# Seven products instead of eight in the first matrix product of the last 1,024 tokens, with the operand sums of two token groups on GpSimd

## The chip, the cores and the metric

The kernel runs on one core of a Trainium2 chip. The core has a matrix engine (TensorE, "PE" in the profile), a vector engine (VectorE, "DVE"), a scalar engine (ScalarE, "ACT"), GpSimd ("POOL") and SyncE ("SP"), all of which run their own instruction streams and meet through semaphores. SBUF is the working memory with 128 partitions, PSUM holds the results of matmuls in eight banks of 128 x 512 float32. DMAs are issued from the queues of POOL, SP and ACT. The metric is the device time of one execution in microseconds (us).

## The reference, cut to what matters

Windowed attention over 8 batches, 8 heads, 576 positions and 64 values a head, and then a two-layer network over all 4,608 tokens:

```python
scores = scale * np.matmul(q, k.transpose(0, 1, 3, 2))
mask = np.abs(pos[:, None] - pos[None, :]) <= 32
scores = np.where(mask, scores, -1000000000.0)
attn = softmax(scores)
x = np.matmul(attn, v).transpose(0, 2, 1, 3).reshape(4608, 512)
h = x @ w_in                # 512 -> 2048: the first product
g = np.maximum(h, 0.0) ** 2
out = g @ w_out             # 2048 -> 512: the second product
```

Inputs and output are float32; the kernel computes in bfloat16 with float32 sums.

## The kernel before, in words

**Attention.** The 576 positions of a batch are cut into three blocks of 192 queries; there are 24 blocks G = 0 to 23. For each block q, k and v are loaded by POOL (`load_qk`, `load_v`, L365 and L396; these DMAs turn float32 into bfloat16), two pieces each. q and k are then transposed: on PE for the first two batches (`turn_pe`, L432), by DMA transposes from SP's queue afterwards (`turn_dma`, L452). `scores` (L489) multiplies them into PSUM region AT, ACT takes the exponential (L510), DVE multiplies by the window's mask (L515), `pv` (L535) multiplies with v, and DVE divides by the row sum (L550, L553). In the first three blocks the mask is added on PE instead (L480). `xturn` transposes the result into the ring XT, on PE for six blocks, by DMA from SP after that (L584, L587).

**First product.** `mm1` (L605) takes a token tile of 192, 256 or 512 tokens and one or two column tiles of 128 of the 2,048, four matmuls for each, into one of two PSUM banks HT. ACT applies relu (L611), DVE squares (L614) into the ring GT. A tile can start only when XT holds all its tokens. Before, tiles have 192 tokens up to 768, 256 up to 1,024 and 512 after that.

**Second product.** For the first 512 tokens it is done plainly (`mm2`, L625). From there on it works in groups g = 1 to 8 of 512 tokens by Strassen's scheme (`strassen`, `product`, L687): seven products P1 to P7 of half size instead of eight. Each is issued as two halves, "a" and "b", of eight matmuls of 256 columns. The operands' sums are made beforehand: those of W2 once (`sums_w2`, L648), those of the tokens for each group (`sums_g`, L663: four sums in two parts, eight DVE instructions of 128 x 1024). The partial results are put together by ACT and DVE (L698, L715, L721, L723, L725), and ACT's queue stores them (L707). There is one set of three sum buffers SS, so the sums of one group wait for the products of the group before; the third sum is written over a quarter of GT.

**The order of the work.** Every operation is recorded by `Prog.rec` with what it reads and writes, a duration that the author booked, and a key. `Prog.schedule` then goes through all engines in simulated time, takes on each the ready operation with the lowest key, and so fixes the order on each engine; DMA queues have booked speeds, shares and slacks (`serve`). Keys come from the token position plus per-block offsets (OG for attention, OL for loads, OS for the second product's groups); DVE's and ACT's keys are taken from when PE needs them (`late`, BIAS). Gaps on PE before 40 us are filled with idle matmuls on zeros (L294). Nothing in the program orders engines apart from the semaphores that follow from reads and writes, and each engine works strictly in the order written down. Loads of batches 2 and later wait for a matmul recorded just before them (`after=self.moe`). The first loads stand in the list `opening()`: the first k by SP, one q by ACT, the others by POOL.

Of the kernel before, what the change touches and what calls it, by code (L numbers as in the profile page):

```python
# [21 lines left out]
BIAS = 74.0  # L22
LS = 10.75
OG = [-0.75, -0.25, -2.0, -2.75, -0.25, 2.25, 4.0, 1.25, 2.0, 1.75, 3.0, 0.75, 0.25, -0.25, -0.5, 0.25, -0.5, -2.0, -2.25, -3.0, 2.75, 1.25, -4.25, 3.0]
OL = [3.0, 1.0, 4.5, 5.5, 2.5, -0.5, -2.0, -3.5, -3.5, -0.5, 0.0, -0.5, -1.0, -3.5, -1.5, 1.5, -0.5, -3.5, -3.5, -1.0, 2.0, 1.0, -3.0, -6.5]
OS = [-4.0, 4.5, -2.0, 2.0, 1.75, 3.25, 4.5, 5.25, 4.5]
NV, NRAW = 6, 6
NTURN = 2
NXT = 6
LEAD = 10.0  # L30
# [5 lines left out]
NSPLIT = 6  # L36
NPM = 3
# [12 lines left out]
class Prog:  # L50
# [11 lines left out]
    def rec(self, eng, fn, reads=(), writes=(), dma=None, dur=100, key=0.0, move=0, name="", after=None, slack=0):  # L62
# [10 lines left out]
        for t in writes:  # L73
            w = self.writer.get(t)
            if w is not None:
                (op.order if w.eng == eng and w.dma is None and dma is None else op.deps).add(w)
            for r in self.readers.get(t, ()):
                (op.order if r.eng == eng and r.dma is None else op.deps).add(r)
# [13 lines left out]
    def schedule(self):  # L92
# [11 lines left out]
        for op in reversed(ops):  # L104
# [3 lines left out]
            if op.eng in ("ACT", "DVE") and op.dma is None and op.key > -50:  # L108
                op.key = op.late / 1000 - BIAS
# [20 lines left out]
        def serve(until):  # L130
            nonlocal now, spent
            while now < until:
# [10 lines left out]
                if spent >= (120 if now < 30000 else 180 if q == "POOL" else 60):  # L143
# [98 lines left out]
def act(n):  # L242
    return 175 + 0.833 * n
# [5 lines left out]

class Gen:  # L250
# [5 lines left out]
    def alloc(self):  # L256
        nc = self.nc
        sb, ps = nc.alloc_sbuf_tensor, nc.alloc_psum_tensor
        self.AT = ps("at", [128, 2048], F32)
        self.HT = [ps(f"ht{i}", [128, 512], F32) for i in range(2)]  # L260
        self.OUTP = [ps(f"outp{i}", [128, 512], F32) for i in range(2)]
# [10 lines left out]
        self.PT = [sb(f"pt{i}", [128, 8, 128], BF16) for i in range(3)]  # L272
# [9 lines left out]
        self.UE = [sb(f"ue{i}", [128, 512], F32) for i in range(2)]  # L282
        self.RT = [sb(f"rt{i}", [128, 512], BF16) for i in range(4)]
# [73 lines left out]
    def load_qk(self, t, b, g, key):  # L357
# [6 lines left out]
        for j in range(2):  # L364
# [4 lines left out]
    def load_hw(self, t, g, eng, cast, key):  # L369
# [4 lines left out]
        for j in range(2):  # L374
            u = 2 * (t == "q") + j
            if g == 0:
                f, tag = self.OE[u][0:h, :], ("oe", u)
            else:
                x = 4 * (g - 1) + u
                f, tag = self.W2[:, 2 * x:2 * x + 2, :].rearrange("p k c -> p (k c)").bitcast(F32)[0:h, :], ("w2f", x)  # L380
# [461 lines left out]
```

## Time and profile before

| | us |
|---|---|
| median of 3 runs (307.56 to 314.36) | 310.13 |
| the profiled execution, whole | 312.76 |
| its span, first to last instruction | 310.8 |
| PE busy | 292.8 |
| DVE busy | 192.6 |
| ACT busy | 166.7 |
| POOL busy | 117.6 |
| mean granted clock of TensorE | 0.995 |

The page divides the span into busy time by engine and by groups of instructions with the same line; an engine's matmul row "x8" stands for eight matmuls in a row, and "idle before" with the name of what ended it. In the view by stage each row is a stretch of the span: its bounds and length, and then the busy time (and number of instructions) of PE, of PE's weight loads, of DVE, ACT and POOL, the granted clock (1.00 is full speed), the share of the DMA engines, and GB/s. POOL's busy time in the kernel before is the issuing of loads, apart from a few small set-up instructions; its last load is issued at 210.5 us.

### The profile page before, as it was taken

What the parts mean: (1) busy time and instruction counts of PE and PEld (TensorE: products, weight loads), DVE (VectorE), ACT (ScalarE), POOL (GpSimd) and SP (SyncE); (2) the same over time, 40 slices, a digit from 0 to 9 for tenths busy, and PEclk for the clock granted to TensorE, in tenths of its full rate; (3) what the DMA queues carried; (4) which work ended last, traced back from release to release, by engine and by line L of the source; (5) the groups of instructions that cost most, each with busy time, mean ns of one, the idle gap of its engine ahead of it and who ended that gap; (6) DMA issues with size and microseconds to landing.
All of it is one profiled execution on the core that took longest, in us unless ns stands there. A gap on an engine that the chain in (4) does not pass through costs nothing.

```text
span 310.8 us, 7401 instructions
## 1 busy us (share of the span) xinstructions
PE 292.8 (94%) x2993; PEld 205.6 (66%) x3027; DVE 192.6 (62%) x420; ACT 166.7 (54%) x260; POOL 117.6 (38%) x153
## 2 busy tenths in 40 slices
PE   6899999999799999999999499999979999999995
PEld 6788776868685567556667455586548556666874
DVE  7135766645986896598539636695549765743701
ACT  3546657747536765746675156625762575355230
POOL 8999457308355650299114002992000000000000
PEclk9999999999999999999999979999999999999999
DMA  9999999999999999999999922999974311201123
GB/s 150 167 206 197 187 153 155 190 170 135 143 169 199 157 161 163 94 151 146 173 144 145 210 41 60 123 156 193 169 97 62 88 41 24 71 34 36 64 71 103
DMA packets 179553, 40.37 MB, mean 130 GB/s; under 512 B 166720, under 2 KB 179008, under 8 KB 179520
## 3 DMA queue, kind: packets, MB, share of 16 engines
q0 software_dynamic: 121920, 18.98, 92.7%
q1 hardware_dynamic: 46752, 11.09, 28.1%
q10 hardware_dynamic: 10848, 9.83, 11.4%
q8 instruction: 24, 0.39, 0.5%
q14 instruction: 9, 0.07, 0.1%
HBM read 38.80 MB, written 9.44 MB: 155 GB/s over the span
## 4 chain that ended last, share of the span: by engine, by line
PE 68%; issue 10%; DMA 8%; POOL 6%; DVE 4%; ACT 1%; SPq 1%; POOLq 0%; ACTq 0%; DVEq 0%
PE ht L605 30%; PE outp L687 23%; DMA kraw<-in_k_dram 5%; PE outp L625 4%; PE at L535 4%; PE at L489 3%; POOL kraw L365 2%; POOL qraw L365 2%; POOL v L396 2%; DMA v<-in_v_dram 2%; DMA qt<-qraw 2%; PE outp L294 2%; DVE ss L663 1%; DVE gt L614 1%; ACT rt L611 1%
## 5 line engine op out<-in xcount | busy, mean ns | idle before, releaser
L605 PE MATMUL ht<-xt,w 128*128 128x512 bf16 (+2 forms) x741 | 136.8, 326 | 6.1 <-issue 4.6
L611 ACT ACTIVATE rt<-ht 128x512 bf16<-128x512 f32 (+1 forms) x152 | 86.5, 576 | 74.4 <-PE ht L605 65.4
L605 PEld LDWEIGHTS ht<-xt,w 128*128 128x128 bf16 x768 | 68.6, 98 | 48.7 <-issue 5.6
L614 DVE TENSOR_TENSOR gt<-rt 128x512 bf16<-128x512 bf16 (+1 forms) x152 | 61.5, 408 | 59.0 <-ACT rt L611 56.6
L365 POOL DMA_DIRECT2D kraw<-in_k_dram x46 | 36.2, 809 | 92.6 <-issue 47.6
L510 ACT ACTIVATE e<-at 128x1024 bf16<-128x1024 f32 x42 | 41.4, 1021 | 11.0 <-PE at L489 11.0
L396 POOL DMA_DIRECT2D v<-in_v_dram x48 | 41.5, 891 | 0.1
L515 DVE TENSOR_TENSOR pt<-e,mask 128x1024 bf16<-128x1024 bf16 x42 | 29.0, 691 | 18.3 <-ACT e L510 18.2
L365 POOL DMA_DIRECT2D qraw<-in_q_dram x46 | 36.3, 810 | 0.5 <-issue 0.5
L687 PE MATMUL outp<-w,gt 128*128 128x256 bf16 x256 | 32.2, 273 | 0.7 <-ACT outp L698 0.7
L687 PE MATMUL outp<-ts,ss 128*128 128x256 bf16 x256 | 31.7, 273 | 0.3 <-DVE ss L663 0.3
L687 PE MATMUL outp<-ts,gt 128*128 128x256 bf16 x256 | 31.6, 273 | 0.0
L687 PEld LDWEIGHTS outp<-w,gt 128*128 128x128 bf16 x256 | 24.7, 98 | 7.7 <-ACT outp L698 1.1
L687 PEld LDWEIGHTS outp<-ts,ss 128*128 128x128 bf16 x256 | 24.4, 98 | 5.9 <-DVE ss L663 0.4
L687 PEld LDWEIGHTS outp<-ts,gt 128*128 128x128 bf16 x256 | 24.6, 98 | 4.2
L535 PEld LDWEIGHTS at<-v,pt 128*64 128x64 bf16 (+1 forms) x576 | 17.1, 106 | 12.6 <-issue 4.2
L535 PE MATMUL at<-v,pt 128*64 128x65 bf16 (+1 forms) x576 | 20.8, 196 | 2.8 <-DVE xa L553 1.7
L550 DVE RECIPROCAL rs<-at 64x8 f32<-64x8 f32 (+1 forms) x48 | 10.0, 209 | 15.3 <-PE at L535 14.0
L489 PEld LDWEIGHTS at<-qt,kt 64*128 64x128 bf16 x384 | 10.8, 94 | 11.1 <-issue 10.5
L489 PE MATMUL at<-qt,kt 64*128 64x128 bf16 x384 | 15.9, 218 | 1.8 <-DMA qt<-qraw 1.8
L553 DVE TENSOR_TENSOR xa<-at,rs 64x512 bf16<-64x512 f32 x24 | 16.7, 695 | 0.8
L553 DVE TENSOR_TENSOR xb<-at,rs 128x512 bf16<-128x512 f32 x24 | 16.5, 689 | 0.7
(65 smaller groups left out, 218.6 us busy)
## 6 DMA issues: line engine op xcount, KB each, us to landing
out_dram<-oe ACTq DMA_DIRECT2D x36, 256.0 KB, 4.5
qraw<-in_q_dram POOLq DMA_DIRECT2D x46, 96.0 KB, 8.6
v<-in_v_dram POOLq DMA_DIRECT2D x32, 128.0 KB, 10.6
w<-in_moe_w_in_dram POOLq DMA_DIRECT2D x4, 512.0 KB, 9.4
w<-in_moe_w_out_dram POOLq DMA_DIRECT2D x4, 512.0 KB, 16.6
kraw<-in_k_dram POOLq DMA_DIRECT2D x14, 112.0 KB, 12.9
kraw<-in_k_dram POOLq DMA_DIRECT2D x16, 96.0 KB, 6.0
v<-in_v_dram POOLq DMA_DIRECT2D x16, 96.0 KB, 12.0
```

What stands on the lines that cost most here:

```text
L365: self.p.rec("POOL", lambda e, j=j: e.dma_start(raw[0:h, j, :].rearrange("p (h d) -> p h d", h=8), s[:, j]), writes=[("raw", t, G % NRAW, ...
L396: self.p.rec("POOL", lambda e, j=j, lo=lo, hi=hi, k0=k0: e.dma_start(vt[lo - k0:hi - k0, j, :, 0:64], self.v[b, :, lo:hi, :].rearrange("h ...
L489: mm = e.matmul(sc[:, 512 * par + 128 * j:512 * par + 128 * j + 128], kt[r:r + 64, j, k0:k0 + 128], q, start=not pm, stop=True, skip_group ...
L510: self.p.rec("ACT", lambda e, e_=e_, sc=sc: e.activation(e_[:], sc, ACTF.Exp, scale=0.125), reads=tags[w], writes=[("e", n % 2)], key=key, ...
L515: self.p.rec("DVE", lambda e, pt=pt, ee=ee, mb=mb: e.tensor_tensor(pt[:], ee, mb, ALU.mult), reads=[("e", n % 2), ("mask", mi)], writes=[( ...
L535: mm = e.matmul(avp[z:z + n, c:c + 65], pt[:, 4 * (h % 2) + h // 2, z:z + n], vt[:, w, h, 0:65], start=((w == 0 or z == 64) and y == 0), s ...
L553: self.p.rec("DVE", lambda e: e.tensor_tensor(x[r0:128, :].rearrange("p (x y c) -> p x y c", x=2, y=4), av[:, :, :, 0:64], rb, ALU.mult), ...
L605: mm = e.matmul(ht[:, n * x:n * x + n], self.W1[:, ft, 128 * d:128 * d + 128], self.XT[:, ft, r:r + n], start=(ft == 0), stop=(ft == 3))
L611: self.p.rec("ACT", lambda e: e.activation(rt[:, 0:c], ht[:, 0:c], ACTF.Relu), reads=[f"ht{k % 2}"], writes=[("rt", k % 4)], key=key, dur= ...
L614: self.p.rec("DVE", lambda e: e.tensor_tensor(gt[:, d0:d0 + len(ds), rg:rg + n], rr, rr, ALU.mult), reads=[("rt", k % 4)], writes=[("gt", ...
L625: mm = e.matmul(op[:], gt[:, d, r:r + 128], self.W2[:, d, :], start=(d == 0), stop=(d == 15))
L687: mm = e.matmul(op[:, 256 * y:256 * y + 256], lhs[:, l0[0] + k, a:a + 128], rhs[:, r0 + k, c0:c0 + 256], start=start and y == 0 and k == 0 ...
```

## The change: what it does

- **First product of tokens 3,584 to 4,607 by Strassen's scheme.** For the two 512-token groups from 3584 and 4096, `mm1_strassen` replaces `mm1`. A block of it covers column tiles d, d + 1, d + 8 and d + 9: seven products of four matmuls of 256 columns, on two PSUM banks x and y, with copies of partial results on ACT (`copy`), adds from PSUM on DVE (`added`) and relu and square as before (`direct`), or in one DVE instruction where the sum is made by DVE (`square` with relu). Group 3584 uses the two HT banks for its four blocks; group 4096 also uses AT's four banks, which attention has left by then (`set_bits` first fills two of them with zeros). The operands' sums of W1 are made by eight DVE instructions (`sums_w1`) into buffers of q and k that are no longer used; those of x by four for each group (`sums_x`).
- **The sums of groups 6 and 7 of the second product** (`sums_g`, 16 instructions of 128 x 1024) move from DVE to POOL.
- **Tiles of 256 tokens** in the first product are used up to token 2,048 instead of 1,024.
- **The opening** is a new list OPEN, piece by piece: one piece each of q and k by ACT and one of q by SP, the rest by POOL, in another order; W1's parts come as 2, 1, 0, 3. Block 0's scores use both AT regions and its first value product the HT banks (SEP, OWN). There are four PT buffers (masked exponentials) instead of three.
- **The last group** (`last`) runs its seven products in another order, with three PSUM banks of AT, and copies and stores the last results in halves, one of them through SP's queue.
- **The order**: new offsets, keys and booked DMA costs and shares, so all engines' order changes; writes after earlier reads or writes of the same engine now wait on the engine's own semaphore on ACT, DVE and POOL (`rec`).

The diff, cut to its core:

```diff
-BIAS = 74.0
-LS = 10.75
...
+BIAS = 68.0
+LS = 7.75
+MSTART = 7
+NFINE = 2048
...
-LEAD = 10.0
+LEAD = 9.5
...
+POOLG = (6, 7)
+SEP = (0,)
+OWN = (0,)
+OPEN = [("k", 1, 1, "POOL"), ("k", 0, 1, "POOL"), ("k", 2, 1, "POOL"), ("v", 0, 1, "POOL"), ("q", 0, 0, "POOL"), ("k", 2, 0, "POOL"),
+        ("v", 1, 1, "POOL"), ("q", 1, 0, "POOL"), ("k", 1, 0, "POOL"), ("q", 2, 1, "ACT"), ("v", 2, 0, "POOL"), ("v", 0, 0, "POOL"),
+        ("k", 0, 0, "ACT"), ("q", 2, 0, "POOL"), ("v", 1, 0, "POOL"), ("q", 1, 1, "POOL"), ("w1", 2, 0, "POOL"), ("w1", 1, 0, "POOL"),
+        ("w1", 0, 0, "POOL"), ("q", 0, 1, "SP"), ("w1", 3, 0, "POOL"), ("w2", 0, 0, "POOL"), ("w2", 1, 0, "POOL"), ("v", 2, 1, "POOL"),
+        ("w2", 2, 0, "POOL"), ("w2", 3, 0, "POOL")]
...
-                (op.order if w.eng == eng and w.dma is None and dma is None else op.deps).add(w)
+                (op.order if w.eng == eng and eng not in ("ACT", "DVE", "POOL") and w.dma is None and dma is None else op.deps).add(w)
             for r in self.readers.get(t, ()):
-                (op.order if r.eng == eng and r.dma is None else op.deps).add(r)
+                (op.order if r.eng == eng and eng not in ("ACT", "DVE", "POOL") and r.dma is None else op.deps).add(r)
...
-                if spent >= (120 if now < 30000 else 180 if q == "POOL" else 60):
+                if spent >= (400 if q == "POOL" else 200):
...
     def scores(self, G, ws):
-        reg = {w: w if len(ws) == 2 else 0 for w in ws}
+        reg = {w: w if len(ws) == 2 or G in SEP else 0 for w in ws}
     def pv(self, G, w):
+        own = G in OWN and not w
+        if own:
+            hi = ["ht0", "ht1"]
...
+                    cc = c + 2048 * (own and z == 64)
+                    mm = e.matmul(avp[z:z + n, cc:cc + 65], pt[:, 4 * (h % 2) + h // 2, z:z + n], vt[:, w, h, 0:65],
...
+    def sums_w1(self, key):
+        w, p = self.W1, self.p
+        self.WS = [[(self.RAW["qk"[i // 2]][2 * (i % 2) + f], [("raw", "qk"[i // 2], 2 * (i % 2) + f, j) for j in range(2)])
+                    for f in range(2)] for i in range(4)]
+        for f in range(2):
+            a11, a21, a12, a22 = w[:, f, 0:1024], w[:, f, 1024:2048], w[:, 2 + f, 0:1024], w[:, 2 + f, 1024:2048]
+            s = [self.WS[i][f][0][:].rearrange("p j c -> p (j c)") for i in range(4)]
+            t = [self.WS[i][f][1] for i in range(4)]
+            w1 = [("w1", d) for d in range(4)]
+            for o, a, b, op, rd, wr in ((s[0], a21, a22, ALU.add, w1, t[0]), (s[1], s[0], a11, ALU.subtract, w1 + t[0], t[1]),
+                                        (s[2], a11, a21, ALU.subtract, w1, t[2]), (s[3], a12, s[1], ALU.subtract, w1 + t[1], t[3])):
+                p.rec("DVE", lambda e, o=o, a=a, b=b, op=op: e.tensor_tensor(o, a, b, op), reads=rd, writes=wr, key=key,
+                      dur=dve(1024), name=f"ws{f}")
+    def set_bits(self, key):
+        for tag, bank in ((self.half(1), 1), (self.half(3), 3)):
+            self.p.rec("PE", lambda e, bank=bank: e.matmul(self.AT[:, 512 * bank:512 * bank + 512], self.ZZ[:, 0:128], self.ZZ[:], start=True,
+                                                      stop=True), reads=["zz"], writes=tag, key=key, dur=216, name="bits")
+    def sums_x(self, t0, key):
+        r, p = t0 % RING, self.p
+        b11, b12, b21, b22 = (self.XT[:, f:f + 2, r + c:r + c + 256] for f in (0, 2) for c in (0, 256))
+        steps = [(t0 // 64 + x) % (RING // 64) for x in range(8)]
+        xt = [("xt", s, x) for s in steps for x in range(2)]
+        x = [t[:] for t in self.XS]
+        for n, o, a, b in ((0, x[0], b12, b11), (2, x[2], b22, b12), (1, x[1], b22, x[0]), (3, x[3], b21, x[1])):
+            p.rec("DVE", lambda e, o=o, a=a, b=b: e.tensor_tensor(o, a, b, ALU.subtract),
+                  reads=xt + ([("xs", n // 2)] if n % 2 else []), writes=[("xs", n)], key=key, dur=dve(512), name=f"x{t0}.{n}")
+    def mm1_strassen(self, t0, d, pair, key):
+        p, gt, w = self.p, self.GT, self.W1
+        r, rg = t0 % RING, t0 % GRING
+        (x, xtag), (y, ytag) = [((self.HT[i][:], [f"ht{i}"]) if pair == 0 else
+                                 (self.AT[:, 512 * (2 * pair - 2 + i):512 * (2 * pair - 2 + i) + 512], self.half(2 * pair - 2 + i)))
+                                for i in range(2)]
+        steps = [[(t0 // 64 + 4 * h + n) % (RING // 64) for n in range(4)] for h in range(2)]
+        xt = [[("xt", s, f) for s in steps[h]] for h in range(2) for f in range(2)]
+        w1 = [("w1", n) for n in range(4)]
+        xb = lambda f, h: (lambda k: self.XT[:, 2 * f + k, r + 256 * h:r + 256 * h + 256])
+        xs = lambda n: (lambda k: self.XS[n][:, k, :])
+        wb = lambda f, h: (lambda k, e: w[:, 2 * f + k, 1024 * h + 128 * e:1024 * h + 128 * e + 128])
+        ws = lambda n: (lambda k, e: self.WS[n][k][0][:].rearrange("p j c -> p (j c)")[:, 128 * e:128 * e + 128])
+        wst = lambda n: self.WS[n][0][1] + self.WS[n][1][1]
+
+        def product(n, k):
+            bank, tag, start, lhs, rhs, rd = {
+                1: (x, xtag, True, wb(0, 0), xb(0, 0), w1 + xt[0]), 2: (x, xtag, False, wb(1, 0), xb(1, 0), w1 + xt[1]),
+                6: (y, ytag, False, ws(1), xs(1), wst(1) + [("xs", 1)]), 5: (x, xtag, True, ws(0), xs(0), wst(0) + [("xs", 0)]),
+                7: (y, ytag, False, ws(2), xs(2), wst(2) + [("xs", 2)]), 3: (x, xtag, False, ws(3), xb(1, 1), wst(3) + xt[3]),
+                4: (y, ytag, False, wb(1, 1), xs(3), w1 + [("xs", 3)])}[n]
+
+            def f(e):
+                for c in range(2):
+                    for z in range(2):
+                        mm = e.matmul(bank[:, 256 * c:256 * c + 256], lhs(z, d + c), rhs(z), start=start and c == 0 and z == 0,
+                                      stop=z == 1, skip_group_check=True)
+                return mm
+
+            self.moe = p.rec("PE", f, reads=rd + ([] if start else tag), writes=tag, key=k, dur=437, name=f"Q{t0}.{d}.{n}")
...
+        def square(i, j, src, tag, k, relu):
+            dst, g = dest(i, j)
+            ss = src.rearrange("p (c t) -> p c t", c=2)
+            if relu:
+                p.rec("DVE", lambda e: e.scalar_tensor_tensor(dst, ss, 0.0, ss, ALU.max, ALU.mult), reads=tag, writes=g, key=k,
+                      dur=dve(512, False), name=f"g{t0}.{d}")
+            else:
+                p.rec("DVE", lambda e: e.tensor_tensor(dst, ss, ss, ALU.mult), reads=tag, writes=g, key=k, dur=dve(512), name=f"g{t0}.{d}")
+
+        def direct(i, j, src, tag, k):
+            n = self.k1
+            self.k1 += 1
+            rt = self.RT[n % 4]
+            p.rec("ACT", lambda e: e.activation(rt[:], src, ACTF.Relu), reads=tag, writes=[("rt", n % 4)], key=k, dur=act(512),
+                  name=f"r{t0}.{d}")
+            square(i, j, rt[:], [("rt", n % 4)], k, False)
+
+        def added(i, j, src, tag, other, otag, k):
+            n = self.kh
+            self.kh += 1
+            hb = self.HB[n % 2]
+            p.rec("DVE", lambda e: e.tensor_tensor(hb[:], src, other, ALU.add), reads=tag + otag, writes=[("hb", n % 2)], key=k,
+                  dur=dve(512, False), name=f"h{t0}.{d}")
+            square(i, j, hb[:], [("hb", n % 2)], k, True)
+
+        u2, p5 = (x[:].bitcast(F32) for x in self.E)
+        ks = [key + 0.25 * n for n in range(7)]
+        product(1, ks[0])
+        copy(y, x, xtag, ytag, ks[0], f"sd{t0}.{d}")
+        product(2, ks[1])
+        direct(0, 0, x, xtag, ks[1])
+        product(6, ks[2])
+        copy(u2, y, ytag, [("e", 0)], ks[2], f"u{t0}.{d}")
+        product(5, ks[3])
+        copy(p5, x, xtag, [("e", 1)], ks[3], f"p{t0}.{d}")
+        product(7, ks[4])
+        added(1, 1, y, ytag, p5, [("e", 1)], ks[4])
+        product(3, ks[5])
+        added(0, 1, x, xtag, u2, [("e", 0)], ks[5])
+        product(4, ks[6])
+        direct(1, 0, y, ytag, ks[6])
...
+                eng = "POOL" if g in POOLG else "DVE"
+                p.rec(eng, lambda e, o=o, a=a, b=b, op=op: e.tensor_tensor(o, a, b, op), reads=rd, writes=wr,
+                      key=key + 0.1 * n, dur=pool(1024) if g in POOLG else dve(1024), name=f"s{n}{g}.{c}")
...
     def strassen(self, g, key):
...
+        if g == NTOK // 512 - 1:
+            self.last(g, ks, out, copy)
+            return
...
+    def last(self, g, ks, out, copy):
...
+        self.product(g, 1, ks[0])
+        for h in range(2):
+            part("ACT", ys[h][0], x[:, c[h]], ["outp0"], ys[h][1], ks[0], f"seed{g}{h}")
+        self.product(g, 5, ks[1])
+        copy(p5, z, zt, [("ue", 1)], f"p5.{g}", ks[1])
+        self.product(g, 2, ks[2])
+        out(0, 0, ["outp0"], lambda e, oe: e.activation(oe[:], x[:], ACTF.Copy), "ACT", ks[2], f"c11.{g}")
+        self.product(g, 6, ks[3])
+        for h in range(2):
+            part("ACT", u2[:, c[h]], ys[h][0], ys[h][1], [("ue", 0, h)], ks[3], f"u2.{g}{h}")
+        self.product(g, 3, ks[4], (0,))
+        self.product(g, 7, ks[4] + 0.2)
+        for h in range(2):
+            u = 4 * g + 3
+            part("DVE", self.OE[u % 4][:, c[h]], ys[h][0], ys[h][1] + [("ue", 1)], [("oe", u % 4, h), ("oe", u % 4)], ks[4],
+                 f"c22.{g}{h}", p5[:, c[h]])
+            store("ACT", 512 * g + 256 + 128 * h, 1, u, h)
+        self.product(g, 3, ks[5] + 0.5, (1,), rds=self.half(2))
+        out(0, 1, zt + [("ue", 0, 0), ("ue", 0, 1)], lambda e, oe: e.tensor_tensor(oe[:], z, u2[:], ALU.add), "DVE", ks[5], f"c12.{g}")
+        for h in range(2):
+            u = 4 * g + 2
+            self.product(g, 4, ks[6], (h,))
+            part(("ACT", "DVE")[h], self.OE[u % 4][:, c[h]], ys[h][0], ys[h][1], [("oe", u % 4, h), ("oe", u % 4)], ks[6],
+                 f"c21.{g}{h}")
+            store(("ACT", "SP")[h], 512 * g + 256 + 128 * h, 0, u, h)
...
     def build(self):
...
-            n = 192 if t0 < 768 else 256 if t0 < 1024 else 512
+            n = 192 if t0 < 768 else 256 if t0 < NFINE else 512
             m = 512 // n
+            if t0 >= 512 * MSTART:
+                if t0 == 512 * MSTART:
+                    at(t0 / 64 - 1, self.sums_w1, t0 / 64 - 1)
+                at(t0 / 64 - 0.5, self.sums_x, t0, t0 / 64 - 0.5)
+                if t0 == NTOK - 512:
+                    at(t0 / 64 - 0.9, self.set_bits, t0 / 64 - 0.9)
+                for x in range(4):
+                    pair = x % 3 if t0 == NTOK - 512 else 0
+                    at(t0 / 64 + 2 * x, self.mm1_strassen, t0, 2 * x, pair, t0 / 64 + 2 * x + OM[pair])
+                t0 += n
+                continue
```

## The prediction

> **What bounds the kernel now.** I read the busy row first, then the chain that ended last, then busy time by stage, then the timeline round the stage where TensorE (PE) is idle.
>
> ```profile
> span 310.8 us, 7401 instructions
> PE 292.8 (94%) x2993; PEld 205.6 (66%) x3027; DVE 192.6 (62%) x420; ACT 166.7 (54%) x260; POOL 117.6 (38%) x153
> PE 68%; issue 10%; DMA 8%; POOL 6%; DVE 4%; ACT 1%; SPq 1%; POOLq 0%; ACTq 0%; DVEq 0%
> ```
>
> PE is busy 94% of the span and is most of the chain. The next view, busy time by stage, says where it is not: at 80 us, at 170 us (with the granted clock at 0.92 and 0.90), at 220 us, and behind the last matmul. VectorE (DVE) works 6 to 7 us in ten at 250 to 270, and GpSimd (POOL) nothing.
>
> ```profile
> 80.00:90.00 10.00, 8.03 (x104) 6.84 (x102) 9.13 (x17) 5.59 (x8) 2.81 (x5) 1.00 1.93 169
> 170.00:180.00 10.00, 5.72 (x66) 4.58 (x65) 6.32 (x12) 1.97 (x3) 0.00 (x0) 0.92 1.38 195
> 180.00:190.00 10.00, 9.95 (x88) 5.76 (x88) 4.67 (x11) 5.80 (x9) 0.00 (x0) 0.90 0.18 46
> 220.00:230.00 10.00, 8.19 (x83) 5.16 (x84) 5.56 (x12) 5.42 (x10) 0.00 (x0) 1.00 1.56 155
> 250.00:260.00 10.00, 9.89 (x83) 5.67 (x79) 6.33 (x14) 6.95 (x12) 0.00 (x0) 1.00 0.12 34
> 260.00:270.00 10.00, 9.95 (x74) 7.06 (x73) 7.08 (x13) 3.73 (x7) 0.00 (x0) 1.00 0.15 42
> ```
>
> The timeline at 170 us: SyncE issues a transpose of x at 170.93; PE's next tile of the first product comes at 179.07 after 4.28 us idle. By the trace's semaphore times that transpose (block 15) landed at 178.49. The tile covers 512 tokens and needs it.
>
> ```profile
> 170.93 1.22 SPq L587 DMA_TRANSPOSE xt<-xb  x1
> 179.07 3.08 PE L605 MATMUL ht<-xt,w 128*128 128x512 bf16 x7 [4.28 <-issue]
> ```
>
> **PE's account.** Laid end to end, matmuls start 0.2155 us apart at 512 columns, 0.109 at 256, 0.082 at 192 (the chain has 4 in 0.86, 8 in 0.87, 8 in 0.66). Before's whole list, without the idle matmuls of L294, comes so to 272.0 us. The last matmul ends at 307.5, so 35.5 are lost: 16.8 by 27.1 us, 2.6 in small pieces to 71, 2.3 at 80 to 85, 1.0 at 107 to 115, 5.8 at 172 to 182 (4.3 idle, the rest at half clock), 1.9 at 223 to 229, and some 5 in pieces of 0.1 to 0.3 at changes of work. Behind the last matmul come 3.3 us, and 2.0 lie outside the span: the execution took 312.76, 2.6 over the median of 310.13.
>
> **Part by part** (against 312.76).
>
> *Matmuls.* Two groups of the first product cost 128 x 0.2155 = 27.6 us; as seven products, 224 x 0.109 = 24.4: -3.2. Tokens 1024 to 2047 in 256-column tiles: 256 x 0.109 instead of 128 x 0.2155, +0.3. Two set_bits matmuls +0.4, eight more small ones for block 0 +0.1. Sum **-2.4**.
>
> *The wait at 172.* The order of the changed kernel puts 17.9 us of PE work between block 15's last value product and the first tile that needs it, 8.1 before. The transpose landed some 12 us after that product; the wait goes: **-5.8**. Next late would be block 18 (11.6, before 10.7) and block 10 (12.2): no wait now at 10.7, so 0.
>
> *The wait at 82.* PE had nothing to run while DVE made group 1's sums, since tile 1024 needed block 7 too (landed 91.16). A 256-column tile needs block 6 only: **-2.0** (0 to -2.3). Block 6 now has 8.1 us of cover; its transpose took 7.5 from the product at 77.0 to 84.5. So 0, up to +2.
>
> *The wait at 229* (scores of block 21 on its transposes): its loads move ahead of blocks 22's and 23's on POOL's queue: **-1** (0 to -1.9). Other blocks' scores come nearer to their loads; no row shows those margins: **+2**, from 0 to 6 (three times the 1.9 seen).
>
> *Opening.* POOL's loads land one after the other: pieces of q and k 0.63 us apart, of v about 0.83, chunks of W1 2.54 (the first issued 11.07, landed 17.76; the fourth 25.4). Now W1's first-needed chunk is third of its kind, behind one piece of q/k and one of v more, and one load less goes over the hardware queues (0.8 us earlier): 17.8 + 1.5 + 5.1 - 0.8 = 23.5, the last 26.1. Blocks 0 and 1 (6.2 us of PE work) are done by then; from 23.5 PE has 3.6 us of tiles by 27.1: 9.8 done against 10.35. **+0.6** (-0.5 to +3, if block 1's attention is not done by 23.5).
>
> *Tail.* The last copy is 256 columns (about 0.42 like L614's row, not 0.60) and its store goes by SyncE: **-0.2**. Waits on the same engine's earlier writes (new in rec): those writes lie several instructions back, 0; if not, 0.07 each for a few dozen, under 2.
>
> *The seven-product blocks.* Each block of two column tiles has, on its first bank, four turns of 0.44 matmul, 0.2 until the reader starts and 0.6 to 0.7 reading: 5.4 us for 3.1 of PE work. The order fills that with second-product halves (0.87 each): PE has 39 us of work over group 3584's four blocks, which need 22. **+1** for more changes of work (0 to 3).
>
> Sum: -2.4 - 5.8 - 2.0 - 1 + 2 + 0.6 - 0.2 + 1 = -7.8: **305.0** if DVE and POOL keep up.
>
> *DVE.* From the end of P5.5 (POOL's first sum waits for it) to P7.7 are 51.6 us of PE work. DVE's queue in it: 16 adds from PSUM, 4 output adds and 4 normalisations at 0.69 and 4 reciprocals at 0.21, together 17.4; and, with both inputs in SBUF, 16 squares at 0.42 and 15 relu-squares (no row at this size: 0.42 of L614 to 0.69 of an add; I take 0.69), 4 masks, 4 x sums: 21.8. Together 39.2 of 51.6: it fits. The eight W1 sums (0.69) stand earlier.
>
> *POOL's sums.* No row has arithmetic on POOL. Bounds: DVE's 0.69, and 3.2 (the iota's 0.228 for 128 elements against 0.10 for one is 1.0 ns an element, for two inputs and one output in turn). I take 2.15: 16 sums are 34 us. Alone they are in time: P6.6 needs five, 10.8 against 16.3 us of PE work ahead of it; P7.6 needs three after the last square, 8.5 against 15.3.
>
> *Beside one another.* No row shows POOL reading SBUF while DVE does. The nearest row is L614 at 421 ns in 130 to 140, where POOL issues loads all ten us, and 423 in 250 to 260 with POOL still: no cost. But those issues read no tile, so it bounds from below only. The other end: a sum and a two-input DVE instruction take turns. The add that frees the bank for block 4 of 3584 stands behind seven two-input instructions; 4.7 + 7 x (2.15 + 0.56) = 23.7 us, while PE wants it at 15.9: 8 late. The second eight sums fall three behind P6.5 (2.6) and five beside the squares of 4096, where the same count makes 7: 10. So 0 to 18. I take **10**, since an instruction that arrives part-way waits less and a late PE spreads DVE's work.
>
> The Trainium skill, SBUF — State Buffer, "Who interferes with whom", says that a DVE instruction with two SBUF inputs contends with a GpSimd instruction that reads SBUF, and "SBUF: two separate sides" that the loser waits for the whole of the other. By it the upper end would hold, 305 + 18 = 323. No trace here shows it. GPSIMD Engine Reference, "3.1 Elementwise", has 4497 ns for 2048 elements with two inputs; half of it, 2.25 (an estimate), would move the sum by under 1 us.
>
> **The forecast: 315 us**, 305 + 10, 1.6% over the median.
>
> **Rivals.**
> - *Side by side:* POOL's sums and DVE do not meet. For it: L614's equal rows. Against: another kind of work. 305, 300 to 306 with the terms' bounds. Chance 0.3.
> - *In turns (forecast):* price 5 to 14, 309 to 319. Chance 0.4.
> - *Full turns, slower:* the place is the adds of 3584's second block; the price 18, and a PE wait of over 4 us brings half clock as at 178 (1.5): 319 to 325. It decides from the point where POOL's sum exceeds DVE's slack per two-input instruction, (51.6 - 39.2) / 39 = 0.3 us held on average, against up to 2.15. Chance 0.2.
> - *The change does not do what it says:* the blocks wait for their own copies (5.4 us against 3.1), and the 3.2 us of matmul come back as gaps: 308 to 311, with the sums harmless. Chance 0.1.
>
> **How the numbers follow.** Faster by over 2% (about what a measurement of this kernel can tell from no change) is under 303.9, slower over 316.3. Faster: two thirds of side by side, 0.2. Slower: all of full turns and a third of the forecast's, 0.34. Within: the rest, 0.46. The range for 8 in 10 goes from 301 (the low end of side by side nearly) to 322 (most of full turns).
>
> **What would show it.** Matmuls of the first product from 3584 on at 256 columns, PE's list at 269.6; no idle over 2 us at 172 and at 82; first tile of the first product at 23 to 24 us instead of 18.6. In turns: POOL's tensor_tensor rows, or DVE's squares next to them, far longer than 0.42 to 0.69 (towards 2 to 3 us), and PE waiting for DVE between 250 and 290. Side by side: squares at 0.42 and 0.69 there, PE at 9.9. The forecast is wrong if DVE's rows keep their lengths, or if new waits for transposes over 6 us appear between 60 and 230 us.

## The result and the profile after

The changed kernel takes **321.38 us** (median of 4 executions, 320.38 to 324.16), the kernel before 312.25 on the same chip (307.56 to 317.19): a ratio of **1.042, 95% interval 1.029 to 1.055**. (A ratio compares only the executions of each kernel that lie within 1.5% of its fastest, here two of the four of before, so it is larger than 321.38 over 312.25.) It is slower. The forecast was 315, 1.6% over the 310.13 known then; the time lies inside the range of 301 to 322, at its upper end, and the case that came true is the one with the chance of 0.2, full turns.

The first lines of the page after, its span, its busy row and the chain that ended last:

```profile
span 322.3 us, 8059 instructions
PE 299.6 (93%) x3291; PEld 230.9 (72%) x3291; DVE 224.0 (70%) x437; ACT 169.1 (52%) x270; POOL 154.0 (48%) x170
PE 75%; DVE 10%; DMA 9%; POOL 4%; issue 2%; ACT 1%; DVEq 0%; ACTq 0%; POOLq 0%
```

TensorE (PE) still has 93%, but DVE's share of the chain rose from 4% to 10%, and DVE is busy 224.0 us against 192.6. Busy time by stage (length of the stretch, then PE, PEld, DVE, ACT and POOL with their instructions, granted clock, DMA share, GB/s) says where:

```profile
80.00:90.00 10.00, 9.70 (x114) 7.87 (x112) 9.47 (x20) 6.47 (x10) 8.84 (x12) 1.00 1.38 132
170.00:180.00 10.00, 10.00 (x101) 6.74 (x100) 8.38 (x18) 5.19 (x8) 5.88 (x8) 1.00 1.94 152
...
220.00:230.00 10.00, 10.00 (x85) 6.79 (x83) 4.50 (x11) 5.34 (x9) 0.00 (x0) 1.00 1.70 168
230.00:235.00 5.00, 3.31 (x39) 2.26 (x37) 3.97 (x3) 1.77 (x3) 3.67 (x2) 1.00 0.04 9
235.00:240.00 5.00, 1.71 (x9) 1.22 (x10) 4.97 (x3) 0.62 (x2) 5.00 (x3) 0.75 0.00 0
240.00:245.00 5.00, 5.00 (x28) 3.70 (x27) 4.10 (x5) 1.94 (x2) 4.56 (x3) 0.57 0.16 52
245.00:250.00 5.00, 4.08 (x44) 3.43 (x41) 4.78 (x6) 1.78 (x3) 4.15 (x2) 1.00 0.18 62
250.00:255.00 5.00, 3.35 (x31) 2.59 (x32) 3.49 (x6) 1.19 (x2) 0.50 (x1) 0.66 0.22 59
...
285.00:290.00 5.00, 3.60 (x32) 2.89 (x32) 4.21 (x5) 2.53 (x5) 4.91 (x3) 1.00 0.00 0
```

The three holes of before, at 80, at 170 and at 220, are closed. New ones stand at 230 to 255 and at 274 to 293, where POOL does its 16 sums. At 235 to 240 DVE completes three instructions and POOL three in 5 us, both "busy" all the time, PE has work for 1.71 us, and its granted clock is 0.75 in that stretch and 0.57 in the next. The timeline of that place, all engines (start, length, engine, line, tiles, count, idle before and who ended it):

```profile
231.33 4.38 POOL L794 TENSOR_TENSOR ss<-gt 128x1024 bf16<-128x1024 bf16 x2 [12.97 <-PE ps L823]
231.37 4.61 DVE L697 TENSOR_TENSOR xs<-xt 128x512 bf16<-128x512 bf16 x2
...
233.78 0.61 PE L725 MATMUL ps<-xs,qraw 128*128 128x256 bf16 x4 [1.07 <-DVE xs L697]
...
235.66 2.30 POOL L794 TENSOR_TENSOR ss<-ss,gt 128x1024 bf16<-128x1024 bf16 x1
235.91 4.59 DVE L697 TENSOR_TENSOR xs<-xt,xs 128x512 bf16<-128x512 bf16 x2
237.92 2.30 POOL L794 TENSOR_TENSOR gt<-gt 128x1024 bf16<-128x1024 bf16 x1
...
238.29 1.04 PE L725 MATMUL ps<-xs,qraw 128*128 128x256 bf16 x4 [3.90 <-DVE xs L697]
```

POOL and DVE start within 0.04 us of one another. DVE's four x sums of tokens 3584 (`sums_x`, the operand sums that the seven-product blocks need) take 9.2 us, one for each of POOL's sums, and PE waits for two of them, 1.07 and 3.90 us. The groups of DVE and POOL from 226 to 300 us (busy, mean ns of one, idle before). L746 are the squares, L743 relu and square in one instruction (relu-squares), L760 the adds from PSUM, L697 the x sums, L531 the masks of attention:

```profile
L746 DVE TENSOR_TENSOR gt<-rt 128x512 bf16<-128x512 bf16 x14 | 15.1, 1080 | 6.5 <-ACT rt L752 6.4
L743 DVE SCALAR_TENSOR_TENSOR gt<-hb 128x512 bf16<-128x512 bf16 x16 | 12.4, 795 | 0.1
L760 DVE TENSOR_TENSOR hb<-ps,e 128x512 bf16<-128x512 f32 x16 | 10.6, 685 | 4.0 <-ACT e L732 3.4 <-PE ps L725 0.5
L697 DVE TENSOR_TENSOR xs<-xt 128x512 bf16<-128x512 bf16 x4 | 6.7, 1711 | 0.0
L697 DVE TENSOR_TENSOR xs<-xt,xs 128x512 bf16<-128x512 bf16 x4 | 5.4, 1345 | 0.0
L531 DVE TENSOR_TENSOR pt<-e,mask 128x1024 bf16<-128x1024 bf16 x4 | 4.1, 1020 | 0.0
...
L794 POOL TENSOR_TENSOR ss<-gt,ss 128x1024 bf16<-128x1024 bf16 x4 | 9.3, 2326 | 1.3 <-PE ps L823 1.3
```

All four groups of DVE with both inputs in SBUF (L746, L743, L697, L531) have grown on average. One by one in the trace, 14 of their 44 instructions took 1.4 to 2.4 us, each of them beside a sum of POOL; the other 30 kept their lengths of about 0.42 and 0.68. The add of L760, one input in PSUM and one in SBUF, has not grown: 685 ns on average, and 0.68 to 0.69 in the four that ran beside a sum.

By the account of the prediction (matmuls laid end to end against the time of the trace), PE's list is 269.6 us, as worked out; 20.3 us are lost by 31.4 (before 17.0 by 30.9), 9.3 more by 231 (before 16.8), and **20.5 from 231 to the last matmul at 319.7 (before 1.8)**. Behind it come 2.6 us and 1.9 outside the span: 324.16 for the profiled execution, 11.4 over that of before. The term that decides is the third: +18.7.

### The profile page after: what moved, and what is told of

The parts are those of the page before. It is cut to its first block, busy times and chain, and to the rows that moved or that the text cites. A ratio compares the mean times of both kernels' runs of the same rounds, so it can differ in the third digit from the quotient of the medians.

```text
span 322.3 us, 8059 instructions
## 1 busy us (share of the span) xinstructions
PE 299.6 (93%) x3291; PEld 230.9 (72%) x3291; DVE 224.0 (70%) x437; ACT 169.1 (52%) x270; POOL 154.0 (48%) x170
## 4 chain that ended last, share of the span: by engine, by line
PE 75%; DVE 10%; DMA 9%; POOL 4%; issue 2%; ACT 1%; DVEq 0%; ACTq 0%; POOLq 0%
PE ps L626 31%; PE ps L823 25%; PE ps L725 6%; DMA xt<-xa 5%; PE ps L646 4%; PE ps L555 4%; DMA w<-in_moe_w_in_dram 4%; PE ps L505 3%; DVE xs L697 3%; DVE gt L746 3%; POOL v L412 1%; POOL kraw L383 1%; DVE hb L760 1%; DVE gt L743 1%; POOL qraw L383 1%
## 5 line engine op out<-in xcount | busy, mean ns | idle before, releaser
L626 PE MATMUL ps<-xt,w 128*128 128x256 bf16 (+2 forms) x768 | 109.1, 291 | 2.7 <-DMA xt<-xa 2.0
L632 ACT ACTIVATE rt<-ps 128x512 bf16<-128x512 f32 (+1 forms) x120 | 67.0, 572 | 59.1 <-PE ps L626 45.0
L626 PEld LDWEIGHTS ps<-xt,w 128*128 128x128 bf16 x768 | 68.5, 98 | 25.7 <-issue 2.2
L526 ACT ACTIVATE e<-ps 128x1024 bf16<-128x1024 f32 x42 | 41.1, 1022 | 8.3 <-PE ps L505 4.7
L531 DVE TENSOR_TENSOR pt<-e,mask 128x1024 bf16<-128x1024 bf16 x42 | 30.1, 721 | 14.1 <-ACT e L526 13.8
L823 PE MATMUL ps<-w,gt 128*128 128x256 bf16 x256 | 33.0, 274 | 1.2 <-DVE oe L862 0.9
L823 PE MATMUL ps<-ts,gt 128*128 128x256 bf16 x256 | 33.1, 277 | 0.0
L823 PE MATMUL ps<-ts,ss 128*128 128x256 bf16 x256 | 31.9, 273 | 0.0
L823 PEld LDWEIGHTS ps<-w,gt 128*128 128x128 bf16 x256 | 24.7, 99 | 6.4 <-DVE oe L862 1.2
L823 PEld LDWEIGHTS ps<-ts,gt 128*128 128x128 bf16 x256 | 24.9, 100 | 4.3
L823 PEld LDWEIGHTS ps<-ts,ss 128*128 128x128 bf16 x256 | 24.4, 98 | 3.7
L746 DVE TENSOR_TENSOR gt<-rt 128x512 bf16<-128x512 bf16 x16 | 15.8, 998 | 6.5 <-ACT rt L752 6.4
L725 PE MATMUL ps<-xs,qraw 128*128 128x256 bf16 x64 | 10.6, 292 | 7.7 <-DVE xs L697 5.5
```

What stands on the lines that cost most here:

```text
L526: self.p.rec("ACT", lambda e, e_=e_, sc=sc: e.activation(e_[:], sc, ACTF.Exp, scale=0.125), reads=tags[w], writes=[("e", n % 2)], key=key, ...
L531: self.p.rec("DVE", lambda e, pt=pt, ee=ee, mb=mb: e.tensor_tensor(pt[:], ee, mb, ALU.mult), reads=[("e", n % 2), ("mask", mi)], writes=[( ...
L626: mm = e.matmul(ht[:, n * x:n * x + n], self.W1[:, ft, 128 * d:128 * d + 128], self.XT[:, ft, r:r + n], start=(ft == 0), stop=(ft == 3))
L632: self.p.rec("ACT", lambda e: e.activation(rt[:, 0:c], ht[:, 0:c], ACTF.Relu), reads=[f"ht{k % 2}"], writes=[("rt", k % 4)], key=key, dur= ...
L725: mm = e.matmul(bank[:, 256 * c:256 * c + 256], lhs(z, d + c), rhs(z), start=start and c == 0 and z == 0, stop=z == 1, skip_group_check=True)
L746: p.rec("DVE", lambda e: e.tensor_tensor(dst, ss, ss, ALU.mult), reads=tag, writes=g, key=k, dur=dve(512), name=f"g{t0}.{d}")
```

## The experiments

The theory, *in turns*: an instruction of DVE with two inputs in SBUF and an operand sum on POOL cannot run together; each waits for the whole of the other. First rival, *own copies*: the seven-product blocks of the first product wait for their own copies and adds, and the sums only happen to stand there. Second rival, *amount of work*: any work of POOL on SBUF does it, whether it reads there or not.

**1. The sums shrunk, nothing else moved.** In four kernels only the instruction that POOL issues for a sum is another; they leave out the sums of groups 6 and 7, or most of them. The planner's durations are the same, so every engine has the same order.

```diff
 # a_tiny
-e.tensor_tensor(o, a, b, op)
+e.tensor_tensor(o[:, 0:1, 0:8], a[:, 0:1, 0:8], b[:, 0:1, 0:8], op)
 # b_half
+e.tensor_tensor(o[:, 0:2], a[:, 0:2], b[:, 0:2], op)
 # c_one_input
+e.tensor_copy(o, a)
 # e_write_only
+e.memset(o, 0.5)
```

> The changed kernel with its instruction order on every engine kept, but each of GpSimd's 16 operand sums cut to 8 elements per partition, so that groups 6 and 7 of the second product get unfinished operands. In turns (DVE's instructions with two inputs in SBUF and GpSimd's sums hold each other off for a whole instruction): TensorE's waits between 231 and 300 us go, x sums at 0.42 us instead of 1.3 to 1.7 and squares at 0.42 instead of 1.00; 20.3 us lost there fall to 2 to 3: 303 to 305. Own copies (a seven-product block waits for its own copies and adds): rows of DVE and GpSimd shrink, but gaps of 10 us or more stay between 231 and 300: 311 or more.

> The same order, each GpSimd sum on half its elements (512 of 1,024 per partition), the other half left out. In turns: a sum takes about 1.1 us instead of 2.2, and every DVE instruction behind one waits half as long, so the 18 us of the two stalls fall to about half or less: 308 to 313. Threshold instead (DVE has 0.3 us to spare per two-input instruction, and the rest is absorbed by slack): 304 to 307. Own copies: 311 or more, with DVE's rows no matter.

> The same order, each GpSimd sum made a copy of its first operand: one input instead of two, the same 1,024 elements written; the sums themselves are left out. If any GpSimd instruction that reads SBUF takes turns with DVE's two-input instructions: DVE's x sums and squares stay at 1 us and over, and the time falls only as the copy is shorter than 2.2 us; with a copy of 1 to 1.2 us as in the run with half the elements, 308 to 313. If only two inputs on GpSimd bring the turns: rows at 0.42 and 303 to 305.

> The changed kernel in its own order, with each GpSimd sum made a memset of the same 1,024 elements, which writes SBUF and reads nothing; the sums themselves are left out. If GpSimd's reading of SBUF is what DVE waits for: x sums and squares back at 0.42 us and 303 to 306, as with the tiny sums. If any GpSimd work on SBUF holds DVE off: squares and x sums at 0.6 us or more next to the memsets, and the time above that of the tiny sums by the memsets' length, as the copies' 1.19 us cost 2.2 us.

Measured, with the changed kernel itself in the first row and the kernel with these sums on DVE (experiment 2) in the last. The columns are the length of one POOL instruction (mean of all 16), DVE's x sums (first kind, second kind) and squares at L746, and the median time. The kernels ran on more than one chip, each in turn with the kernel before, so the last column is the one to compare:

| POOL does | POOL, us | x sums, us | squares (mean of 16), us | time, us | ratio to before |
|---|---|---|---|---|---|
| sums, 2 inputs, 1024 elements | 2.26 | 1.71, 1.35 | 1.00 | 321.4 | 1.042 |
| half a sum, 512 | 1.28 | 0.90, 0.86 | 0.61 | 309.0 | 0.992 (0.986 to 0.998) |
| copy, 1 input, 1024 | 1.17 | 0.84, 0.81 | 0.54 | 307.4 | 0.989 (0.984 to 0.994) |
| memset, no input, 1024 | 0.95 | 0.42, 0.42 | 0.42 | 306.8 | 0.989 (0.978 to 1.000) |
| tiny sums, 8 | 0.25 | 0.42, 0.43 | 0.42 | 305.2 | 0.984 (0.973 to 0.994) |
| nothing (sums on DVE) | none | 0.42, 0.42 | 0.42 | 305.4 | 0.982 (0.969 to 0.995) |

The rows behind it, groups of 226 to 300 us (POOL's from 200 us). Tiny sums:

```profile
L760 DVE TENSOR_TENSOR hb<-ps,e 128x512 bf16<-128x512 f32 x16 | 10.5, 684 | 4.4 <-ACT e L732 2.6 <-PE ps L725 1.7
L746 DVE TENSOR_TENSOR gt<-rt 128x512 bf16<-128x512 bf16 x16 | 6.6, 421 | 7.0 <-ACT rt L752 6.8
...
L697 DVE TENSOR_TENSOR xs<-xt 128x512 bf16<-128x512 bf16 x4 | 1.5, 423 | 0.0
```

The copy with one input:

```profile
L746 DVE TENSOR_TENSOR gt<-rt 128x512 bf16<-128x512 bf16 x16 | 8.6, 544 | 6.4 <-ACT rt L752 6.2
...
L697 DVE TENSOR_TENSOR xs<-xt 128x512 bf16<-128x512 bf16 x4 | 3.2, 837 | 0.0
...
L794 POOL COPY ss<-gt 128x1024 bf16<-128x1024 bf16 x8 | 9.4, 1191 | 35.8 <-PE ps L823 31.2 <-DVE gt L743 4.6
```

The memset:

```profile
L746 DVE TENSOR_TENSOR gt<-rt 128x512 bf16<-128x512 bf16 x16 | 6.6, 420 | 7.0 <-ACT rt L752 6.9
...
L697 DVE TENSOR_TENSOR xs<-xt 128x512 bf16<-128x512 bf16 x4 | 1.5, 420 | 0.0
...
L794 POOL MEMSET ss<- 128x1024 bf16 x12 | 11.2, 951 | 35.7 <-DVE gt L746 16.9 <-PE ps L823 14.0 <-DVE gt L743 4.7
```

*Own copies* falls: with the same blocks in the same order, tiny sums give back 16 us, and 1.9 us are lost from 231 to the end where the changed kernel lost 20.5. *Amount of work* falls too, by the rows: the memset keeps POOL busy 0.95 us on the same 1,024 elements, nearly as long as the copy, and DVE's rows do not move; the copy reads SBUF, and the x sums double, while the squares go from 0.42 to 0.54. The medians of these two kernels are too close to tell them apart (both 0.989). The traces do: PE's matmuls come in the same order in all five kernels with POOL instructions, and from the first matmul of the seven-product blocks (L725) to the last of the kernel they take 73.6 us with tiny sums, 73.6 with memsets, 76.1 with copies, 78.8 with half sums and 92.2 with whole ones (one execution each). So it is POOL's reading of SBUF that holds DVE off, and one input is enough. The Trainium skill, SBUF — State Buffer, "Who interferes with whom", says that a DVE instruction with two SBUF inputs contends with a GpSimd instruction that reads SBUF and not with one that only writes it, and that a DVE instruction with at most one SBUF input, outside the modes in which it uses two ports, does not contend: by the memset's 0.42 and by L760's 685 ns the trace agrees. In size the copy did less than expected (0.8 us for the x sums and 307.4 us in all, where 1 us and over and 308 to 313 were expected), and the tiny sums and the memsets came 0.2 and 0.8 us above their ranges.

The price is not in proportion to the length: over the tiny ones, sums of half the length cost 3.8 us by the medians and 5.2 by the traces, whole ones 16.2 and 18.6. From the rows: the changed kernel's DVE instructions are 21.2 us longer in all than with tiny sums (squares 16 x 0.577, relu-squares 16 x 0.110, x sums 4 x 1.288 and 4 x 0.917, masks 4 x 0.337); with half sums 7.1, with copies 5.4. By the traces 18.6 of the 21.2 reached the end, 5.2 of the 7.1 and 2.4 of the 5.4: the order took in 2 to 3 us each time, and the rest was lost.

**2. The sums back on DVE.**

```diff
-POOLG = (6, 7)
+POOLG = ()
```

> The whole change but for its last part: the sums of groups 6 and 7 stay on DVE (POOLG empty), all else as changed; the planner places them anew. In turns: no GpSimd arithmetic, DVE's rows at 0.42 and 0.69; DVE has 16 x 0.69 = 11 us more of work in stretches that had about 40 of 52: 303 to 308, faster than before. Own copies: 313 or more, and DVE's 11 us make it no better than the change.

**305.37 us** (304.0 to 307.45): 16 us faster than the changed kernel and, by a ratio of 0.982 (0.969 to 0.995), faster than before. DVE carries the 16 sums at 0.69 us each, 11 us more, and still keeps up. Busy time by stage of this kernel, where the changed one had its holes:

```profile
240.00:250.00 10.00, 9.43 (x114) 7.66 (x112) 9.38 (x19) 6.67 (x11) 0.00 (x0) 1.00 0.27 74
...
270.00:280.00 10.00, 9.57 (x87) 8.10 (x86) 8.89 (x17) 7.13 (x14) 0.00 (x0) 1.00 0.08 26
```

DVE is busy 8.9 to 9.4 us in ten and completes 17 to 19 instructions (11 in the changed kernel at 270 to 280), and PE loses half a microsecond in each. The rest of the change, taken together, gains; the part on GpSimd costs more than the rest brings.

**3. The part on GpSimd alone, in the kernel before.** Its operand sums of groups 6 and 7 on POOL, the planner told 2.25 us.

```diff
-p.rec("DVE", ... e.tensor_tensor(o, a, b, op) ..., dur=dve(1024)
+p.rec("POOL" if g in (6, 7) else "DVE", ..., dur=2250 if g in (6, 7) else dve(1024)
-if op.eng in ("ACT", "DVE") and op.dma is None and op.key > -50:
+if op.eng in ("ACT", "DVE", "POOL") and op.dma is None and op.key > -50:
```

> The kernel before, with one part of the change alone: the operand sums of groups 6 and 7 on GpSimd (declared to the planner at 2.25 us). In turns, whatever the first product does: 16 sums of 2.2 us hold DVE off for some 36 us; a square there takes up to 2.3 us where TensorE needs one per 1.7 us, so 16 squares cost about 0.5 us each beyond what the two buffers hide: 4 to 10 us more than before, 317 to 323. If it takes the seven-product blocks with their x sums to be hurt: within 1% of before.

**323.11 us** (322.52 to 325.59), ratio 1.044 (1.033 to 1.055): as slow as the whole change, without one seven-product block in the first product. By the ratio that is some 13 us over before, more than the 4 to 10 expected. The groups of 226 to 300 us, the first row of the kernel before, the others of this one:

```profile
L614 DVE TENSOR_TENSOR gt<-rt 128x512 bf16<-128x512 bf16 x37 | 15.6, 424 | 17.8 <-ACT rt L611 16.8 <-PE outp L687 0.7
...
L614 DVE TENSOR_TENSOR gt<-rt 128x512 bf16<-128x512 bf16 x38 | 31.2, 837 | 19.6 <-ACT rt L611 11.8 <-POOL ss L663 7.7
L515 DVE TENSOR_TENSOR pt<-e,mask 128x1024 bf16<-128x1024 bf16 x6 | 6.6, 1116 | 4.2 <-ACT e L510 4.2
L663 POOL TENSOR_TENSOR gt<-gt 128x1024 bf16<-128x1024 bf16 x4 | 9.4, 2365 | 0.0
```

The plain squares of L614 go from 424 to 837 ns on average: ten of them, those beside POOL's sums, took 1.2 to 2.3 us, the others 0.41 to 0.43. Here *own copies* cannot be it: there are none. By the account, from 228 us on 13.1 us are lost, where before lost 1.8 from 231 on.

**4. Where it costs.** In the first kernel below, POOL's sums of group 6 wait until DVE has made the x sums of tokens 3584; PE's order is the same. In the second only group 7's sums are on POOL.

```diff
 # i_x_sums_first
-reads=rd
+reads=rd + ([("xs", x) for x in range(4)] if g == 6 else [])
 # j_group7_only
-POOLG = (6, 7)
+POOLG = (7,)
```

> The changed kernel, with GpSimd's sums of group 6 made to wait until DVE has made the four x sums of tokens 3584 to 4095; TensorE's order is the same. In turns, with the place found in the trace (the four x sums take 9.2 us beside the first four GpSimd sums, TensorE waits for them at 233 and 238): they take 1.7 us, the 5 us of wait and its half-clock go, other DVE instructions still wait behind GpSimd's sums: 321.4 - 6 to 7.5 = 314 to 315.5. If the loss follows only the number of GpSimd sums, wherever they stand: 320 to 322.

> The changed kernel with the sums of group 6 back on DVE and only those of group 7 on GpSimd (POOLG of 7 alone). In turns, with a price for each stretch as in the trace (12.7 us lost at 231 to 256, 7.6 at 265 to 300, of which 1.7 stay without any sums): 305.4 + 6.5 to 7 = 312. If each sum costs the same 1.0 to 1.1 us (16 to 18 us over 16 sums): 8 sums, 313.5 to 314.

The first gave **318.03 us** (314.98 to 319.36; ratio 1.018, 1.008 to 1.027), by the medians 3.4 less, half of the expected gain. The execution with the trace took 314.98, 9.2 less than the profiled one of the changed kernel: 2.7 from ahead of the place (by 220 us) and 6.5 from there on. Its timeline:

```profile
228.59 0.76 DVE L697 TENSOR_TENSOR xs<-xt 128x512 bf16<-128x512 bf16 x2
229.27 0.88 DVE L697 TENSOR_TENSOR xs<-xt,xs 128x512 bf16<-128x512 bf16 x2
...
234.40 5.10 POOL L794 TENSOR_TENSOR ss<-ss,gt 128x1024 bf16<-128x1024 bf16 x2
...
234.91 2.60 DVE L531 TENSOR_TENSOR pt<-e,mask 128x1024 bf16<-128x1024 bf16 x1
...
243.08 0.45 PE L555 MATMUL ps<-v,pt 128*64 128x65 bf16 x16 [3.33 <-DVE xa L574]
```

The x sums take 1.6 us instead of 9.2, and PE no longer waits for them. But now the masks of the next block take 2.60 and 2.00, and PE waits 1.47 and 3.33 for them and for the normalisation queued behind: the wait went to the next instruction in DVE's queue. The other three executions were 2.6 to 4.4 us longer, at granted clocks of 0.984 to 0.995 against 1.0; no trace shows them. So the place is worth 3 to 6.5 us of 16, less than it looked in the trace of the changed kernel.

The second gave **313.93 us** (ratio 1.007, 1.003 to 1.011): 8.5 over the kernel without POOL sums. Half the sums, half the price, as the version with 1.0 to 1.1 us for each sum expected; the price by stretch gave 2 less.

**5. The other parts, with the sums on DVE.**

```diff
 # g_no_mm1_seven
-MSTART = 7
+MSTART = 9
 # h_old_opening (l_old_loads_new_banks: OPEN alone)
-OPEN = [("k", 1, 1, "POOL"), ("k", 0, 1, "POOL"), ("k", 2, 1, "POOL"), ("v", 0, 1, "POOL"), ("q", 0, 0, "POOL"),
+OPEN = [("k", 0, 0, "SP"), ("k", 0, 1, "SP"), ("q", 0, 0, "POOL"), ("q", 0, 1, "POOL"), ("k", 1, 0, "POOL"),
...
-SEP = (0,)
-OWN = (0,)
+SEP = ()
+OWN = ()
 # k_512_tiles
-NFINE = 2048
+NFINE = 1024
```

> The changed kernel without seven-product blocks in the first product (MSTART 9) and with all operand sums on DVE. By the account of matmuls these blocks save 3.2 us and cost 0.4 for the zeros and 1 for their changes of work, so without them 1.8 us more than with them (305.4 measured with the sums on DVE): 307, ratio to before 0.988 against 0.982. If the blocks pay nothing: the same 305 or less.

> The changed kernel with the sums on DVE and the opening's order of loads of the kernel before (the same pieces and queues, the score and value products of block 0 in their old banks); all other constants as changed. The prediction had the new opening at +0.6 us; the trace of the changed kernel has 20.1 us lost when the first product starts at 26.3 us, where before lost 16.8 by 27.1. If the order of loads makes that: 302 to 303, ratio 0.973 to 0.975. If the pace of the loads does, whatever their order: 305.

> The changed kernel with the sums on DVE and the opening's loads in the order of the kernel before, but block 0's scores and value product in the changed kernel's banks. If the new banks save what the later first chunk of W1 costs (the run with both old gave 305.07, with both new 305.4): 304 to 304.5. If the banks do nothing: 305.

> The changed kernel with all sums on DVE and tokens 1024 to 2047 in tiles of 512 again (NFINE 1024). By the prediction's term the wait at 82 us comes back, +2.0, and 0.3 of matmul goes: 307, ratio to before 0.988. If the move of loads alone took that wait away: 305.1 or less.

Without seven-product blocks in the first product: **307.12 us** (306.06 to 310.94), 1.7 over the kernel with them, as the account had it (1.8); PE's list is 272.3 instead of 269.6. The intervals overlap, so the time alone does not settle it. (With the blocks goes the filling of the banks that the last group's products add into, so a part of that group's output is left unfinished; the instructions timed are the same.)

Old opening: **305.07** (304.9 to 305.16). Old loads with the new banks: **305.51** (305.25 to 306.08). Against 305.37 with the new opening, nothing. In the traces the old order does lose about 1 us less by 30 us (18.2 against 19.2), which does not appear at the end.

Tiles of 512 tokens again: **308.13** (306.17 to 308.98). The time is near the expected 307, but the trace (of the execution of 306.17) does not have the cause: at 80 to 90 us PE is busy 9.51 us of ten, with no idle over 0.30. So the wait at 82 stays away without the smaller tiles, and whether these 2 to 3 us of time belong to the tiles is open.

The fastest times are those of the changed kernel with all sums on DVE, 305.1 to 305.5 with either opening: 1.6 to 2.1% under before.

## Why the prediction was right or wrong

Against the profiled executions the forecast was 315.0 and the changed kernel took 324.16; 9.2 us are to be placed: +8.6 in the price of the turns, +2.7 in the opening, -0.9 in the blocks, -0.7 in the waits and -0.6 in the tail.

- **Beside one another, the price of 10: the step that failed, by size.** Named rightly, priced by half: 0 to 18 was the range, 10 was taken, and 18.6 came (20.5 lost from 231 on, less 1.9 with tiny sums). The two reasons given for taking less than the upper end bought little. "An instruction that arrives part-way waits less": that was so for six of the 14 that were held (1.4 to 1.9 us each), but POOL's sums stand back to back, and DVE's next instruction was mostly waiting already when one ended, so the other eight took 2.0 to 2.4 us, one for each sum. "A late PE spreads DVE's work": DVE's order is fixed, and a two-input instruction that waits holds the adds behind it, for which PE and ACT wait (from 270 to 300 us ACT waited 3.0 us and PE 1.6 us for the adds of L760). The slack of 12.4 us (51.6 less 39.2) was also read wrongly: a sum over a stretch does not tell how much waiting a fixed order can take in. 21.2 us of added DVE time cost 18.6, not 21.2 less 12.4; what the order could take in was 2 to 3 us. (Two of the sums are off by their own figures, and nothing hangs on either: the two-input instructions come to 21.5, not 21.8, and the three sums that P7.6 needs to 6.5, not 8.5.)
- **Full turns, slower (0.2): what happened, in another place.** Its 319 to 325 holds 321.4 and 324.2. Its place, the adds of 3584's second block, was wrong: the four x sums at 231 came first. Its half clock was there, and longer than the 1.5 us named: 0.75 at 235 to 240, 0.57 at 240 to 245, 0.66 at 250 to 255. Its point of decision, 0.3 us held on average, is no threshold: over the 44 instructions with two inputs in SBUF, copies held DVE 0.12 us on average and half sums 0.16, and by the traces both already cost time (2.4 and 5.2 us); whole sums held it 0.48 and cost 18.6.
- **POOL's sum at 2.15: right.** 2.12 alone, 2.30 beside a DVE instruction of 0.42. The Trainium skill's GPSIMD Engine Reference, "3.1 Elementwise", gave 2.25 by halving its figure, which is for float32 (an estimate).
- **Side by side (0.3), 305.0: right as a sum, and not as the mechanism.** Without POOL's reads the time is 305.2 (tiny sums), 305.4 (sums on DVE) and 306.8 (memsets, 304.9 to 308.0). The opening, 2 us too small there, was made up by the blocks, the tail and the waits (below): errors that cancelled, which is luck.
- **Opening +0.6: a term mis-sized.** It cost +3.3 in the changed kernel's trace and about +2.2 in that with sums on DVE. The row:

```profile
26.33 1.49 PE L626 MATMUL ps<-xt,w 128*128 128x192 bf16 x16 [0.68 <-DMA w<-in_moe_w_in_dram]
```

The first tile came at 26.33, not 23 to 24. The third chunk of W1 was indeed the one needed, 5.1 us behind the first; but the first landed at 21.19, 3.4 us later than before, where the prediction had 0.7. With the sums on DVE it landed at 20.10 in this order of loads and at 17.96 in the old one, so the order accounts for some 2 us of that landing. But the old order did not make the kernel faster, so no more than the trace's 1 us hangs on that order.
- **Waits at 172, 82 and 229 gone, new ones +2: right.** From 31 to 231 us 7.5 less was lost than before, against -6.8 worked out. Block 15's and block 21's waits are gone; one new wait, 1.71 us at 148 for a transpose, is the +2. For the wait at 82 the sum was right and the cause not: it goes without the 256-column tiles too.
- **Matmuls -2.4: right**, 269.6. **The blocks' own +1: too much**, 0.1 by the trace with tiny sums (1.9 lost from 231 on, before 1.8). **Tail -0.2:** it was -0.8, 4.5 behind the last matmul to the end of the execution against 5.25.
- **The chances.** Slower had 0.34. Given that the nearest row for POOL beside DVE (loads beside squares, 421 ns) "read no tile", as the prediction says itself, it bore on nothing that POOL's sums do, and the middle of 0 to 18 had no row of its own behind it.

## What to carry to other kernels

Moving elementwise work to GpSimd does not take it off VectorE if the GpSimd instruction reads SBUF and VectorE's instructions have both inputs there: price each such GpSimd instruction as a stretch in which VectorE gets one two-input instruction done, whatever their lengths, and count VectorE's instructions there, not its free microseconds. If VectorE stands on the path in that stretch, take the sum of these waits as lost but for what the order can take in (2 to 3 us here); moving one victim away exposes the next one in the queue, and brought half of what was expected. Before giving up a change, time its parts apart: here all but the part on GpSimd was together a gain of 1.8%.

## What the runs showed of the hardware

- A copy with one SBUF input on GpSimd holds VectorE's two-input instructions off as a sum does, for its shorter length (x sums 0.82 us beside copies of 1.17); a memset of the same elements, 0.95 us, does not: of the 44 instructions 15 ran beside a memset, and none was longer for it (x sums 0.42).
- "Two inputs in SBUF" includes the same tile read twice: the square of L746 reads `rt` for both and went from 0.42 to as much as 2.3 us. An add with one of its inputs in PSUM kept its 0.69 beside the same sums.
- GpSimd waits as well, by VectorE's length less about 0.24 us: a sum takes 2.12 alone, 2.30 beside instructions of 0.42 and 2.56 to 2.57 beside those of 0.69 (the masks and relu-squares of experiment 4).
- On GpSimd a sum of 1,024 bfloat16 elements takes 2.12 us, a copy 1.13 to 1.19, a memset 0.95; VectorE's sum takes 0.68.
